# Moving the first two loads of k to ScalarE's DMA queue, with alpha's first load ahead on SyncE's

## The chip, the cores and the metric

The kernel runs on one core of a Trainium2 chip. A core has a matrix engine (TensorE, "PE" in the profile, with its weight loads as "PEld"), VectorE ("DVE"), ScalarE ("ACT"), GpSimd ("POOL") and SyncE ("SP", which in this kernel only starts transfers). Every engine works through its own instructions in order, and the engines wait for one another by semaphores. Sixteen DMA engines move data between the chip's main memory and the on-chip memory; a transfer is started by an instruction on the queue of SP, ACT or POOL.

The metric is the device time of one execution in microseconds (us). Three runs of the kernel before took 187.92, 188.28 and 188.16 us; the median is 188.16 us.

## The reference

Two stages follow one another. The first is a recurrence over 768 steps for each of 4 batches and 8 heads, with heads 48 wide; the second is a two-layer network on its output, with 3072 rows, 384 columns and 2048 hidden columns.

```python
def _attn_ref(q, k, v, alpha):
    state = zeros(B, H, D, D)
    for t in range(S):
        state = alpha[:, :, t, :, None] * state + einsum('bhd,bhe->bhde', k[:, :, t], v[:, :, t])
        y[:, :, t] = einsum('bhd,bhde->bhe', q[:, :, t], state)
def _moe_ref(x, w_in, w_out):
    h = x @ w_in
    return (h * cos(h)) @ w_out
```

## The kernel before, in words

The sequence of each batch is cut into three stretches of 256 steps. There are so 12 stretches, which the code calls pairs and numbers J = 0 to 11. Within a pair the 256 steps lie on 128 partitions, two steps each (e = 0 and 1), so that each of the four inputs of a pair is one tile of 128 x 768 numbers, 384 KB, brought in by one transfer. Its rows are pieces of 384 bytes (two steps of one head).

What happens to a pair, with the lines:

- `load` (L102) brings one input of one pair. Every load goes through `nc.sync.dma_start` (L105), so all 48 of them stand in one order on SP's queue.
- `ln` (L139) takes the logarithm of alpha on ACT. Ahead of the first `ln` the function `act_set` (L134, L136) loads the table that holds logarithm and exponential; it is ACT's first instruction.
- `cums0` and `cums` (L174, L158, both through L155) build running sums of the logarithms on PE.
- `icp` and `exps` (L189, L194) take exponentials of these sums on ACT; `scale_k` (L212) and `scale_q` (L216) multiply k and q by them, on DVE for pairs 0 and 1.
- `cast_v` (L219) rounds v on POOL; `decay` (L244) prepares decay factors there, and behind these stand the loads of the network's weights w1 and w2 (L121, L127), which POOL's queue starts.
- PE then transposes (L260), forms scores (L274), outer products (L291) and the recurrence's output (L340); after that the pair's 256 rows go through the two layers, `mlp1` (L361), cosine on ACT (L367), product on DVE (L372) and `mlp2` (L390).
- `idle` (L416) puts matmuls of zeros on PE in the beginning, at seven fixed places of PE's order. Sixteen of them stand ahead of PE's first useful matmul.

The order of everything is written out by hand. `PLAN` (from L433) has a line for each kind of step and a word for each pair: a number, and after a colon the engine. The numbers are only sort keys: all steps are sorted by them, and each engine gets its instructions in that order. Nothing waits until such a time. A gate of its own holds the alpha load of pair 2 back until the recurrence's output of pair 1 is computed (`GATES`, L99), and all later loads of SP stand behind it.

In the beginning SP's queue has, in order: k of pair 0, alpha of 0, alpha of 1, k of 1, v of 0, q of 0, q of 1, v of 1. ACT's order is: table load, `ln` of pair 0, `ln` of pair 1, `icp` of (0, 0), `exps` of (1, 0), `icp` of (1, 1), `icp` of (0, 1), and so on. DVE's scalings of k come in the order (0, 0), (1, 1), (0, 1), (1, 0), where the pair stands first and e second.

Of the kernel before, what the change touches and what calls it, by code (L numbers as in the profile page):

```python
# [16 lines left out]
def kernel(  # L17
# [10 lines left out]
    nc = tc.nc  # L28
# [65 lines left out]
    w1 = consts.tile([C, KT, DF], BF, tag="w1", name="w1")  # L94
    w2 = consts.tile([C, NF, DM], BF, tag="w2", name="w2")
# [3 lines left out]
    GATES, AFTER = {("a", 2): ("yT", 1)}, {}  # L99
    src = {"a": alpha, "k": k, "q": q, "v": v}  # L100

    def load(nm, J):  # L102
        b, g = J // NJB, J % NJB
        t = sb.tile([C, H, 2, D], FP, tag=nm, name=nm, bufs=BUF["a" if nm == "a" else "in"])
        dma = nc.sync.dma_start(  # L105
            out=t.rearrange("p h e d -> p h (e d)"),
            in_=src[nm][b, :, g * T2 : (g + 1) * T2, :].rearrange("h (p e) d -> p h (e d)", e=2),
        )
        if (nm, J) in AFTER:
            tc.add_manual_dep(dma.ins, AFTER[nm, J].ins.name,  # L110
                              mybir.DependencyInfo(mybir.DependencyClass.Sync, mybir.DependencyReason.DATA),
                              reason="inputs of later pairs stay behind the weights")
        if nm == "a":
            a_sb[J] = t
        else:
            kqv[nm, J] = t
# [295 lines left out]
    def idle(n):  # L412
# [5 lines left out]
    copies = {"DVE": nc.vector.tensor_copy, "ACT": nc.scalar.copy}  # L418
    mults = {"DVE": nc.vector, "POOL": nc.gpsimd}
    steps = {  # L420
        "load": lambda J, nm: load(nm, J), "w1": load_w1, "w2": load_w2,
        "mula": mul_a, "ln": ln, "cums0": cums0, "cums": cums, "sub": sub, "icp": icp, "exps": exps, "eb": session,
        "sk": lambda J, e, eng="POOL": scale_k(J, e, mults[eng]), "sq": lambda J, e, eng="POOL": scale_q(J, e, mults[eng]),
        "castv": cast_v, "vst": stack_v, "vpe": stack_v_pe,
# [7 lines left out]

    PLAN = {  # L433
# [68 lines left out]
    for key, line in PLAN.items():  # L502
        kind, *rest = key.split()
        for J, word in enumerate(line.split()):
            if word != "-":
                t, _, eng = word.partition(":")
# [38 lines left out]
```

## Time and profile before

| what | value |
|---|---|
| median of three runs | 188.16 us (187.92 to 188.28) |
| profiled execution: span from first to last instruction | 186.5 us, granted PE clock 1.000 |
| PE busy | 176.7 us, 95% of the span |
| DVE, ACT, POOL busy | 135.4, 126.5, 77.1 us |
| the first eight loads, data moving | from about 1.8 to 14.2 us of the span |
| PE's first useful matmul (L155), first matmul of the network (L361) | 7.12 us, 22.20 us |

Of the profiled execution the page gives the span alone, so its own time is not known more closely than that: the median of the timed runs is 1.66 us longer than the span, and that is taken for what lies around it.

Times in the trace are counted from the start of the span. A line of a timeline begins with start and duration of a group of instructions; in brackets stands how long the engine was idle before it and what ended that. A line of the chain has start, duration and the work that the end of the execution can be followed back through. For a transfer the duration on its queue is only the time that the starting instruction took; how long it was until the data had landed is told apart from that.

### The profile page before, as it was taken

Reading aid. Unit: us, or ns where it says so; the run is one execution under the profiler, and the core shown is the slowest. Engines: PE = TensorE matmul, PEld = TensorE weight load, DVE = VectorE, ACT = ScalarE, POOL = GpSimd, SP = SyncE. Lnnn points to the kernel's source line nnn. Section 1 sums busy time; section 2 is a strip of 40 time slices with the busy share of each in tenths; the row PEclk is TensorE's granted clock in tenths of the full one; section 3 lists DMA queues with packets and bytes.
Section 4 is the critical chain, followed back from the end, with each engine's and each line's share of the span. In section 5 each row is a group of like instructions: output and inputs, shape, how many; then the busy total and the mean of one; then the engine's idle time right before and its main releaser. Section 6 shows DMA issues by size and latency. Waiting matters only on the chain.

```text
span 186.5 us, 5746 instructions
## 1 busy us (share of the span) xinstructions
PE 176.7 (95%) x2467; PEld 126.4 (68%) x2469; DVE 135.4 (73%) x184; ACT 126.5 (68%) x161; POOL 77.1 (41%) x110
## 2 busy tenths in 40 slices
PE   7988799989989999999999999999999999999993
PEld 2434588655667786785688668676867686786872
DVE  7178775589799979698847987794977556754461
ACT  2466876889498986889668999728965264373330
POOL 5079510257645653781896076930360320100000
PEclk9999999999999999999999999999999999999999
DMA  6999999999949979996799932600041005301102
GB/s 152 261 258 165 181 204 237 259 266 265 274 105 304 264 180 245 264 260 167 186 278 278 247 104 46 182 0 4 4 136 47 5 0 158 118 0 66 64 0 84
DMA packets 60137, 29.47 MB, mean 158 GB/s; under 512 B 51024, under 2 KB 60112, under 8 KB 60112
## 3 DMA queue, kind: packets, MB, share of 16 engines
q1 hardware_dynamic: 56256, 25.86, 57.2%
q0 software_dynamic: 3712, 3.15, 11.0%
q8 instruction: 19, 0.31, 0.7%
q10 hardware_dynamic: 144, 0.10, 0.2%
q14 instruction: 6, 0.05, 0.1%
HBM read 25.17 MB, written 4.72 MB: 160 GB/s over the span
## 4 chain that ended last, share of the span: by engine, by line
PE 73%; ACT 15%; DVE 8%; issue 3%; DVEq 0%
PE h_ps L361 31%; PE o_ps L390 24%; PE idle_ps L416 4%; PE y_ps L340 3%; ACT qkT L266 3%; DVE gsb L372 3%; PE T_ps L260 2%; ACT c_sb L367 2%; PE A_ps L274 2%; ACT L136 2%; ACT cp L200 2%; PE U_ps L291 2%; DVE kh L212 2%; ACT icp L192 2%; PE o_last L384 1%
## 5 line engine op out<-in xcount | busy, mean ns | idle before, releaser
L372 DVE TENSOR_TENSOR gsb<-h_ps,c_sb 128x1024 bf16<-128x1024 f32 x48 | 58.1, 1221 | 21.9 <-ACT c_sb L367 21.2
L367 ACT ACTIVATE c_sb<-h_ps,halfpi 128x1024 bf16<-128x1024 f32 x48 | 53.0, 1113 | 26.8 <-PE h_ps L361 23.0
L361 PE MATMUL h_ps<-xT,w 128*128 128x256 bf16 x576 | 66.7, 273 | 1.3 <-ACT xT L351 0.7
L390 PE MATMUL o_ps<-w,gsb 128*128 128x384 bf16 x368 | 66.7, 327 | 0.1
L361 PEld LDWEIGHTS <-w 128*128 128x128 bf16 x576 | 55.6, 98 | 10.1 <-issue 1.6
L390 PEld LDWEIGHTS <-gsb 128*128 128x128 bf16 x368 | 33.8, 98 | 21.2 <-DVE gsb L372 0.6
L313 POOL TENSOR_TENSOR un<-us,c 128x384 bf16<-128x384 f32 x20 | 16.7, 835 | 40.7 <-DVE us L305 29.1
L279 DVE TENSOR_TENSOR A_sb<-A_ps,msk 128x1024 bf16<-128x1024 f32 x24 | 28.9, 1215 | 1.7 <-PE A_ps L274 1.7
L212 POOL TENSOR_TENSOR kh<-k,icp 128x384 bf16<-128x384 f32 x17 | 16.9, 999 | 9.2 <-ACT icp L192 7.8
L216 POOL TENSOR_TENSOR qh<-q,cp 128x384 bf16<-128x384 f32 x15 | 15.0, 1006 | 11.8 <-ACT cp L200 11.8
L149 POOL TENSOR_TENSOR a<-a 128x384 f32<-128x384 f32 x9 | 9.0, 1001 | 12.6 <-DMA a<-in_alpha_dram 12.6
L219 POOL CAST vp<-v 128x768 bf16<-128x768 f32 x12 | 10.1, 841 | 8.8 <-DMA v<-in_v_dram 7.7
L416 PE MATMUL idle_ps<-zeros 128*128 128x512 bf16 x38 | 12.0, 457 | 1.4 <-DVE zeros L52 1.2
L141 ACT ACTIVATE lna<-a 128x768 bf16<-128x768 f32 x12 | 10.2, 847 | 4.6 <-DMA a<-in_alpha_dram 4.6
L266 ACT COPY qkT<-T_ps 128x1024 bf16<-128x1024 bf16 x8 | 8.0, 1015 | 6.9 <-PE T_ps L260 4.4
L136 ACT ACT_TABLE_LOAD x9 | 11.5, 1283 | 0.9 <-PEq L529 0.7
L367 ACT ACT_TABLE_LOAD x9 | 11.5, 1283 | 0.2
L266 DVE COPY qkT<-T_ps 128x1024 bf16<-128x1024 bf16 x16 | 10.8, 678 | 1.1 <-ACT qkT L266 1.1
L305 DVE TENSOR_TENSOR us<-U_ps,un 128x384 f32<-128x384 f32 x16 | 8.7, 550 | 3.8 <-PE U_ps L291 2.8
L402 DVE COPY o_sb<-o_ps 128x384 f32<-128x384 f32 x12 | 6.6, 551 | 6.5 <-PE o_ps L390 6.5
L351 ACT CAST xT<-y_ps 128x384 bf16<-128x384 f32 x12 | 6.7, 594 | 5.6 <-PE y_ps L340 3.8
L351 DVE CAST xT<-y_ps 128x384 bf16<-128x384 f32 x12 | 6.8, 584 | 4.7 <-PE y_ps L340 2.9
(69 smaller groups left out, 159.1 us busy)
## 6 DMA issues: line engine op xcount, KB each, us to landing
k<-in_k_dram SPq DMA_DIRECT2D x12, 384.0 KB, 6.0
a<-in_alpha_dram SPq DMA_DIRECT2D x12, 384.0 KB, 6.1
v<-in_v_dram SPq DMA_DIRECT2D x12, 384.0 KB, 6.0
q<-in_q_dram SPq DMA_DIRECT2D x12, 384.0 KB, 6.3
out_dram<-o_sb SPq DMA_DIRECT2D x23, 192.0 KB, 2.6
vs<-vp SPq DMA_DIRECT2D x36, 64.0 KB, 2.1
w<-in_moe_w_out_dram POOLq DMA_DIRECT2D x4, 384.0 KB, 10.1
w<-in_moe_w_in_dram POOLq DMA_DIRECT2D x4, 384.0 KB, 7.3
```

The lines of the kernel that those rows point to most:

```text
L136: nc.scalar.preload_act_table_set("natural_log_exp_and_others")
L212: eng.tensor_tensor(out=kh_t[J % NQ][:, e, :, 0:D], in0=kqv["k", J][:, :, e], in1=icp_, op=ALU.mult)
L216: eng.tensor_tensor(out=qh_t[J % NQ][:, e, :, 0:D], in0=kqv["q", J][:, :, e], in1=cp, op=ALU.mult)
L266: copy(out=qkT_sb[J][:, c], in_=T_ps[J][:, c].rearrange("r n e s -> r n (e s)"))
L279: nc.vector.tensor_tensor(out=A_sb[J][:, c].rearrange("s a p t -> s (a p) t"), in0=A_ps.pop((J, c)).rearrange("s a p t -> s (a p) t"), in1 ...
L313: nc.gpsimd.tensor_tensor(out=u, in0=U_sum.pop(n), in1=c2_sb[J][:, :, c].unsqueeze(3).to_broadcast([C, NP, 2, D]), op=ALU.mult)
L351: copy(out=xT[J][:, :, c * C : (c + 1) * C].rearrange("r i (t e) -> r i e t", e=2), in_=y_ps[J][:, c, 0 : KT * C].rearrange("r (i e t) -> ...
L361: nc.tensor.matmul(h_ps[J, u][:, f, :], w1[:, kk, ft * C : (ft + 1) * C], xT[J][:, kk, :], start=(kk == 0), stop=(kk == KT - 1))
L367: nc.scalar.activation(out=c_sb[J, u], in_=h_ps[J, u], func=AF.Sin, bias=halfpi, scale=1.0)
L372: nc.vector.tensor_tensor(out=gsb[J][:, u * FW : (u + 1) * FW], in0=h_ps.pop((J, u)), in1=c_sb.pop((J, u)), op=ALU.mult)
L390: nc.tensor.matmul(o_ps[J, c][:, 0:DM], gsb[J][:, ft, c * C : (c + 1) * C], w2[:, ft], start=(ft == 0), stop=(ft == NF - 1))
L416: nc.tensor.matmul(idle_ps[0], zeros[:, 0:C], zeros, start=True, stop=True)
```

## The change

`load` takes an engine as a third argument, and the plan's words for the first two loads of k name ACT and carry sort keys below every other load. In SP's order these two drop out, so that it reads: alpha of 0, alpha of 1, v of 0, q of 0, q of 1, v of 1. ACT's order begins with k of 0, k of 1, then the table load, then what it had before. The other ten loads of k stay on SP where they were.

```diff
-    def load(nm, J):
+    def load(nm, J, eng="SP"):
         b, g = J // NJB, J % NJB
         t = sb.tile([C, H, 2, D], FP, tag=nm, name=nm, bufs=BUF["a" if nm == "a" else "in"])
-        dma = nc.sync.dma_start(
+        dma = {"SP": nc.sync, "ACT": nc.scalar}[eng].dma_start(
...
-        "load": lambda J, nm: load(nm, J), "w1": load_w1, "w2": load_w2,
+        "load": lambda J, nm, eng="SP": load(nm, J, eng), "w1": load_w1, "w2": load_w2,
...
         "load a": "1320 1974 27415 27985 34270 40270 43270 54870 67336 68770 70970 93397",
-        "load k": "750 2544 28555 37270 46270 52480 58570 69470 72470 85140 91627 113474",
+        "load k": "750:A 760:A 28555 37270 46270 52480 58570 69470 72470 85140 91627 113474",
         "load q": "5250 6750 29125 38770 48970 56370 57870 60070 78470 84570 87104 96187",
         "load v": "3750 8250 35770 41770 51910 61570 67906 73970 75470 85710 95267 96757",
```

## The prediction

> **What bounds the kernel now.** I read the page first, then the chain of waits in its beginning, then the timelines of ACT, DVE and POOL there, then the landing times of the first loads, and last which DMA queue moved packets when.
>
> ```profile
> span 186.5 us, 5746 instructions
> PE 176.7 (95%) x2467; PEld 126.4 (68%) x2469; DVE 135.4 (73%) x184; ACT 126.5 (68%) x161; POOL 77.1 (41%) x110
> ```
>
> PE is busy for 95% of the span, so a shift of PE's work in the beginning reaches the end unless a gap takes it up. The chain shows what the beginning waits for (start, duration, work):
>
> ```profile
> 1.20 6.09 PE idle_ps L416 x16
> 7.28 0.65 PE cums_h L155 x4
> ...
> 8.11 0.24 PE idle_ps L416
> ...
> 8.36 0.81 PE cums_h L155 x4
> ...
> 9.39 0.49 ACT cp L200
> 9.88 0.39 ACT icp L192
> ...
> 10.29 1.67 DVE kh L212 x2
> ...
> 12.01 0.47 PE U_ps L291 x14
> ...
> 14.35 1.01 ACT qkT L266
> ```
>
> The reader sees a chain of computing with no load in it. Until 7.28 it is PE's own zero matmuls, then the running sums of pair 0, then those of pair 1 at 8.36, then exponentials, scalings of k, outer products. How close the loads come to it is told by the timelines of ACT (three lines) and POOL (one):
>
> ```profile
> 0.74 1.28 ACT L136 ACT_TABLE_LOAD   x1 [0.74 <-PEq L529]
> 5.96 0.84 ACT L141 ACTIVATE lna<-a 128x768 bf16<-128x768 f32 x1 [3.94 <-DMA a<-in_alpha_dram]
> 7.47 0.84 ACT L141 ACTIVATE lna<-a 128x768 bf16<-128x768 f32 x1 [0.66 <-DMA a<-in_alpha_dram]
> 10.50 1.04 POOL L219 CAST vp<-v 128x768 bf16<-128x768 f32 x1 [7.31 <-DMA v<-in_v_dram]
> ```
>
> The logarithm of pair 1 ends at 7.47 + 0.84 = 8.31, and the sums that read it start at 8.36, just as PE's own zero matmul ends (8.11 + 0.24 = 8.35). So alpha of pair 1 has no slack at all, and nothing to give either: landing earlier, it would find PE occupied until 8.35. Alpha of pair 0 has some: its logarithm ends at 6.80, and PE reaches the sums at 7.12 by the timeline.
>
> **Landing times.** A load's landing is the start of its instruction on SP plus its time to landing, which for the loads in turn is 3.7, 4.7, 5.6, 6.1, 6.3: k of 0 at 0.74 + 3.7 = 4.44; alpha of 0 at 1.25 + 4.7 = 5.95; alpha of 1 at 1.86 + 5.6 = 7.46; k of 1 at 2.90 + 6.1 = 9.00; v of 0 at 4.18 + 6.3 = 10.48. They land 1.5 us apart, and 384 KB in 1.5 us is the 261 GB/s that the DMA engines move without a break from 4 to 13 us. So these transfers are bound by the rate of the DMA engines, not by when they are issued.
>
> **The change part by part.**
>
> Two issues leave SP. The first load of k took 0.44 us there; alpha's first is issued at 0.74 instead of 1.25 and alpha's second about 0.5 us earlier. An issue blocked by full queues costs nothing here, since SP does nothing else.
>
> Two issues enter ACT ahead of the table load. Unblocked ones took 0.37 to 0.57 us, so 0.9 us; if the second is held up like the fourth on SP (1.24), 1.7 us. The table load then ends at 0.74 + 0.9 to 1.7 + 1.28 = 2.9 to 3.7, where ACT otherwise sits idle until 5.96 (the 3.94 us in the row above). Cost nothing; the cover is 3.9 us, and would be gone only if alpha of 0 landed before 3.7. The earliest that the rows allow is 4.44, by taking k's place.
>
> k of 0 may land up to 8.69, where the `icp` that DVE waits for ends (8.72 is the start of the scaling); k of 1 up to about 10.27. Landing 1.5 us later than before, at 5.95, k of 0 costs nothing.
>
> v of 0, q and v of 1 are fifth to eighth in bytes before and after, and land as before: 0. POOL and its weight loads hang on `cast_v` and on ACT's exponentials, so they move only with the chain.
>
> Alpha of 1 is the term that counts. Before, SP's order gave the rate to k0, alpha0, alpha1, k1 one after the other. After, two queues ask at once. If the DMA engines serve both evenly, alpha0 and k0 are both done when two transfers' bytes have moved (5.95, as before), and alpha1 and k1 when four have: at 9.00 instead of 7.46, +1.54. From both sides: nothing, if alpha's queue gets enough more than its half (rival 1), down to -0.01, since PE's zero matmul ends 0.01 before the sums start; +1.54 when served evenly or when k goes first. The trace of before never has two hardware queues with a long backlog, so I take the nearest rows: POOL's queue (q0) beside SP's (q1), when the gated alpha load of pair 2 was issued at 27.24 into a backlog of weights. Windows 28 to 28.5, 30.5 to 31 and 31 to 31.5, by queue:
>
> ```profile
> q0 software_dynamic: 132, 0.10, 129.6%
> ...
> q0 software_dynamic: 119, 0.09, 115.1%
> q1 hardware_dynamic: 40, 0.02, 13.9%
> ...
> q1 hardware_dynamic: 257, 0.10, 77.3%
> q0 software_dynamic: 46, 0.03, 35.4%
> ```
>
> The newcomer got nothing until the older backlog ended, some 2.4 us later than the 1.1 us that the very first load needed from issue to first packet. So what was queued earlier goes first. Here both queues start at 0.74 and hand over at the same pace, so by this row, too, their transfers are served side by side. The small lead that either queue may have moves alpha of 1 by some tenths: I take 8.9 and +1.4 of at most 1.54.
>
> [...]
>
> How the +1.4 travels. ACT works in order, so behind the late logarithm `icp` of (0, 0) moves from 8.22 to 9.6, and `exps` of (1, 0), which waits for PE's sums of pair 1, from 9.39 to 10.8. DVE's scalings move with them (10.29 to 11.7), and the outer products end 1.4 later: the wait of 0.49 us for `cast_v` lies ahead of a wait for DVE and hides none of it. From there to the network's first matmul at 22.20 every link is one of computing; POOL starts its weights behind exponentials that have moved too, and the next alpha load hangs on PE's output of pair 1. From 22.2 us on PE has few gaps: in the stretch from 58.9 to 140.0 it is busy for 80.05 of 81.1 us, and no load ends a PE wait. So nothing gives the 1.4 us back, and nothing adds to it: 186.5 + 1.4 = 187.9 for the span, and with the 1.66 us around it 189.56, which I round to 189.6; the median of the runs before is 188.16. A difference of 0.2% (0.38 us) is about what a measurement of this kernel can tell from no change.
>
> **The rivals.**
>
> 1. No change (the other side). Alpha's queue is served first in whole transfers: alpha0, k0, alpha1, k1. Then alpha1 lands at 7.46 as before, k1 at 9.00, alpha0 at 4.44 and nothing uses its 1.5 us, as PE's zero matmuls last until 7.28. Time: 188.16, at best 188.1. It decides from the point where alpha1 lands by 7.84 (0.38 late); while two transfers of alpha move, k's queue may then move 1.25, so alpha needs 62% of the rate. For it: transfers already queued went first in the rows above, and SP's issue of a store took 0.33 us against ACT's 0.37 at the end of the kernel, so alpha might arrive first. Against: a lead of hundredths is no lead of a whole transfer of 1.5 us. The same result comes if two queues together move 320 GB/s in place of 261; SP's queue alone did 319 for one microsecond (3 to 4) and fell back to 262. [...]
>
> 2. k goes first: order k0, k1, alpha0, alpha1. Alpha0 lands at 7.46 and alpha1 at 9.00. The sums of pair 0 then start at 7.46 + 0.84 + 0.05 = 8.35, those of pair 1 at 9.89: +1.53, 189.7. It can't be told from my forecast by the time, but by the first `ln`.
>
> 3. SP's queue is served until empty, as q0 was. SP refills its own (one issue each 1.44 us), so k of 0 would come only behind six transfers, at about 4.44 + 6 x 1.51 = 13.5, and k of 1 at 15.0. The scaling (0, 1) stands behind (1, 1) on DVE and would end near 16.3 instead of 11.96: +4.3, 192.5; somewhere between if k gets a small share. For it: the rows of q0 and q1. Against: there the backlog was 4 transfers old, here both start empty.
>
> 4. A gain. Alpha's and v's earlier landing would have to shorten the chain, and no link of it before 22 us waits for a load; over 0.2% would need 0.38 us from somewhere else.
>
> **How the numbers follow.** Even sharing or k first (mine and rival 2): 0.65, at 189.2 to 189.8. Rival 3: 0.08, at 190 to 192.5. Rival 1: 0.18, at 188.0 to 188.4. A total rate somewhat above 261, so that alpha1 comes 0.4 to 0.9 late: 0.04, at 188.6 to 189.1. A gain: 0.05. Slower by over 0.2%: 0.65 + 0.08 + 0.04 = 0.77; same 0.18; faster 0.05. Leaving out the gain and most of rival 3, the range is 188.0 to 190.6; my own case alone has 189.2 to 189.8.
>
> **What would show it.** Right: the first `ln` still starts near 5.9, the second near 8.9 with some 2 us of idle time behind "DMA a" ahead of it; the sums of pair 1 start near 9.8; the first matmul of the network near 23.6; queues q1 and q10 both move packets from 2 to 8 us. The table load ends before 4 us. Wrong: the second `ln` starts at 7.5 or before (rival 1), the first one at 7.5 (rival 2), or the first scaling of k waits for a transfer of k past 10 us (rival 3). The forecast also falls if the shift is there at 9.8 us but smaller at the end, since then a gap that I took for computing was hiding slack.

## The result, and the profile after

The changed kernel takes 189.54 us (median of five runs, 189.32 to 190.07) against 188.28 us for five runs of the kernel before: 1.0064 times as long, with a 95% interval of 1.0046 to 1.0082. The bound for "no change" was 0.2%, so it is slower, by about 1.2 us. The predicted 189.6 us holds for the total; it does not hold for how the total comes about.

The profiled execution has a span of 187.9 us, 1.4 us more than before. Its head on the page, the two queues that matter from the list of DMA queues (packets, megabytes, share of the sixteen engines' time; q1 is SP's, q10 the new one of ACT):

```profile
span 187.9 us, 5747 instructions
PE 176.3 (94%) x2467; PEld 126.3 (67%) x2469; DVE 134.7 (72%) x184; ACT 126.6 (67%) x161; POOL 76.9 (41%) x110
...
q1 hardware_dynamic: 54176, 25.07, 55.0%
...
q10 hardware_dynamic: 2224, 0.88, 2.1%
```

No engine does noticeably more work than before (ACT 0.1 us), and DVE does 0.7 us less. So the time is in waits. The timeline of ACT in the changed kernel, from the start of the span:

```profile
0.74 1.25 ACTq L105 DMA_DIRECT2D k<-in_k_dram  x2
2.02 1.28 ACT L136 ACT_TABLE_LOAD   x1 [2.02 <-issue]
5.42 0.84 ACT L141 ACTIVATE lna<-a 128x768 bf16<-128x768 f32 x1 [2.12 <-DMA a<-in_alpha_dram]
8.78 0.84 ACT L141 ACTIVATE lna<-a 128x768 bf16<-128x768 f32 x1 [2.52 <-DMA a<-in_alpha_dram]
```

The table load is 1.28 us later and nothing asks for it before 5.42. The second logarithm starts at 8.78 where it started at 7.47: alpha of pair 1 is 1.31 us late. The chain that ends last now begins with that very transfer (start, duration, what):

```profile
0.75 0.44 SPq L105
...
1.25 7.51 DMA a<-in_alpha_dram
8.78 0.85 ACT lna L141
...
9.67 0.81 PE cums_h L155 x4
...
16.52 0.56 DVE us L305
...
17.21 0.40 PE A_ps L274 x8
...
23.31 2.79 PE h_ps L361 x24
```

Before, this chain ran through PE's own zero matmuls up to 8.36 and had no load in it. Now it is issue, transfer, logarithm, sums. How far each place of it has moved, read from the two timelines of PE:

| place | before | after | later by |
|---|---|---|---|
| running sums of pair 1 (L155) | 8.36 | 9.67 | 1.31 |
| last outer product of pair 0 ends (L291) | 12.48 | 13.15 | 0.67 |
| transposes of pair 0 (L260) | 13.67 | 14.43 | 0.76 |
| first scores of pair 0 (L274) | 16.11 | 17.21 | 1.10 |
| first matmul of the network (L361) | 22.20 | 23.31 | 1.11 |
| the network's matmuls near 96 us | 95.89 | 96.98 | 1.09 |
| PE goes on after a short stop near 100 us | 99.39 | 100.71 | 1.32 |

So the shift is not carried whole. 0.55 us of it comes back within about five microseconds, by the transposes, 0.34 us is lost again at the scores, and 0.2 us near 100 us. The sum, 1.31 - 0.55 + 0.34 + 0.23 = 1.33, is close to the 1.4 us of the span. Rows of DVE and PE show the middle steps. First DVE, in the kernel before and, below the dots, in the changed one:

```profile
10.29 2.14 DVE L212 TENSOR_TENSOR kh<-k,icp 128x384 bf16<-128x384 f32 x3 [1.01 <-ACT icp L192]
...
10.03 0.56 DVE L212 TENSOR_TENSOR kh<-k,icp 128x384 bf16<-128x384 f32 x1 [5.49 <-ACT icp L192]
11.60 1.50 DVE L212 TENSOR_TENSOR kh<-k,icp 128x384 bf16<-128x384 f32 x3 [1.01 <-ACT icp L192]
```

The group of three scalings took 2.14 us before and takes 1.50 now. Before, POOL's cast of v ran beside it (10.50 to 11.54). v of pair 0 lands at nearly the same time (0.19 us later), so the cast now lies ahead of the three:

```profile
10.68 0.82 POOL L219 CAST vp<-v 128x768 bf16<-128x768 f32 x1 [7.49 <-DMA v<-in_v_dram]
```

Both are shorter apart (1.50 and 0.82 us) than they were together (2.14 and 1.04 us). This is what comes back: the three start 1.31 us later and end 0.67 us later, at 13.10 for 12.43. The outer products end 0.05 us behind them in both kernels. PE's rows for them, before and, below the dots, after:

```profile
11.59 0.22 PE L291 MATMUL U_ps<-vp,kh 64*128 64x96 bf16 x2 [0.49 <-POOL vp L219]
12.01 0.47 PE L291 MATMUL U_ps<-vp,kh 64*128 64x96 bf16 x14 [0.20 <-DVE kh L212]
...
12.34 0.81 PE L291 MATMUL U_ps<-vp,kh 64*128 64x96 bf16 x16
```

The waits of 0.49 us for the cast and of 0.20 us for DVE are gone, but that by itself gives nothing back. The sixteen now start at 12.34 right behind the eight zero matmuls, and their end, at 13.15, still comes just behind the last scaling.

The loss at the scores is seen in PE's row there, before and, below the dots, after:

```profile
16.11 0.40 PE L274 MATMUL A_ps<-qkT 48*128 48x128 bf16 x8 [0.62 <-ACT vs L239]
...
17.21 0.40 PE L274 MATMUL A_ps<-qkT 48*128 48x128 bf16 x8 [0.96 <-DVE us L305]
```

Before, this wait was 0.62 us and ended with ACT's copy of v (`vs`, L239). That copy is 0.76 us later, so that by it the scores could have started at 16.87. They now start behind DVE's state sum (L305), which ends at 17.07.

### The profile page after: what moved, and what is told of

It reads as the page before. It is cut to its first block, busy times and chain, and to the rows that moved or that the text cites. A ratio compares the mean times of both kernels' runs of the same rounds, so it can differ in the third digit from the quotient of the medians.

```text
span 187.9 us, 5747 instructions
## 1 busy us (share of the span) xinstructions
PE 176.3 (94%) x2467; PEld 126.3 (67%) x2469; DVE 134.7 (72%) x184; ACT 126.6 (67%) x161; POOL 76.9 (41%) x110
## 4 chain that ended last, share of the span: by engine, by line
PE 68%; ACT 15%; DVE 8%; DMA 4%; issue 3%; SPq 0%; DVEq 0%
PE h_ps L361 31%; PE o_ps L390 24%; DMA a<-in_alpha_dram 4%; PE y_ps L340 3%; DVE gsb L372 3%; ACT cp L200 3%; ACT c_sb L367 2%; ACT qkT L266 2%; PE T_ps L260 2%; PE A_ps L274 2%; ACT L136 2%; DVE qh L216 2%; ACT icp L192 2%; ACT lna L141 2%; PE U_ps L291 2%
## 5 line engine op out<-in xcount | busy, mean ns | idle before, releaser
L361 PE MATMUL h_ps<-xT,w 128*128 128x256 bf16 x576 | 66.7, 273 | 1.5 <-ACT xT L351 0.7
L361 PEld LDWEIGHTS <-w 128*128 128x128 bf16 x576 | 55.7, 98 | 10.3 <-issue 1.9
L313 POOL TENSOR_TENSOR un<-us,c 128x384 bf16<-128x384 f32 x20 | 16.9, 846 | 40.9 <-DVE us L305 33.0
L266 DVE COPY qkT<-T_ps 128x1024 bf16<-128x1024 bf16 x16 | 10.7, 676 | 1.1 <-ACT qkT L266 1.1
L305 DVE TENSOR_TENSOR us<-U_ps,un 128x384 f32<-128x384 f32 x16 | 8.7, 549 | 3.8 <-PE U_ps L291 2.8
L274 PE MATMUL A_ps<-qkT 48*128 48x128 bf16 x192 | 9.2, 218 | 1.3 <-DVE us L305 1.0
```

The costliest lines, as they stand in the source:

```text
L266: copy(out=qkT_sb[J][:, c], in_=T_ps[J][:, c].rearrange("r n e s -> r n (e s)"))
L274: nc.tensor.matmul(A_ps[J, c][:, a, p, :], qkT[r, c, NP + p, :], qkT[r, c, p, :], start=True, stop=True)
L313: nc.gpsimd.tensor_tensor(out=u, in0=U_sum.pop(n), in1=c2_sb[J][:, :, c].unsqueeze(3).to_broadcast([C, NP, 2, D]), op=ALU.mult)
L361: nc.tensor.matmul(h_ps[J, u][:, f, :], w1[:, kk, ft * C : (ft + 1) * C], xT[J][:, kk, :], start=(kk == 0), stop=(kk == KT - 1))
```

## Experiments

The theory: two queues share one rate. Alpha of pair 1 is done only when k's transfers have had their half, and the chain waits for this one transfer alone; that ACT issues anything, that k lands later and that the table load is late cost nothing. Rivals: something about the second queue itself costs time (its start, or waits that the build puts elsewhere), the late table load does, or the time is lost after the sums.

### Both loads of k behind alpha, all on SP's queue

```diff
-        "load k": "750:A 760:A 28555 ...",
+        "load k": "1980 2544 28555 ...",
```

> All four loads stay on SP, in the order alpha0, alpha1, k0, k1; nothing on ACT's queue. My theory (alpha of 1 was late because the two queues share the rate): alpha0 lands near 4.4, alpha1 near 5.9, k0 near 7.5, k1 near 9.0; the sums of pair 1 start at 8.0 to 8.4 as PE's zero matmuls allow, and the time is that of before, 188.0 to 188.6. Rival, the order does it (k behind alpha comes too late for DVE): first scaling of k waits for a transfer, slower by over 0.4 us. Rival, ACT's queue does it: the time of before as well.

Measured: 188.37 us against 188.48, ratio 0.9989 (0.9970 to 1.0008), no change. ACT's timeline:

```profile
4.65 0.84 ACT L141 ACTIVATE lna<-a 128x768 bf16<-128x768 f32 x1 [2.62 <-DMA a<-in_alpha_dram]
6.16 0.84 ACT L141 ACTIVATE lna<-a 128x768 bf16<-128x768 f32 x1 [0.67 <-DMA a<-in_alpha_dram]
```

Alpha of pair 1 lands 1.3 us earlier than before, and k of pair 0 3.2 us later (at 7.66 for 4.44; k of pair 1 at about 9.1, as before). Neither shows in the time. The sums of pair 1 started at 8.66, not at the expected 8.0 to 8.4, since the first sixteen zero matmuls ended at 7.76 in this execution (before, 7.29). So k's lateness is free, and with PE's zeros and the order of work as they are alpha has nothing to gain below 7.5.

### Only k of pair 0 on ACT's queue

```diff
-        "load k": "750:A 760:A 28555 ...",
+        "load k": "750:A 2544 28555 ...",
```

> Only k0 goes to ACT's queue; SP has alpha0, alpha1, k1. My theory: alpha0 and k0 share the rate and land near 5.4 to 5.9, then alpha1 has it alone and lands near 7.4, k1 near 9.0; second logarithm near 7.5, time of before, 188.0 to 188.6. Rival, each issue on ACT ahead of the table load costs: about half of the loss, 188.9.

Measured: 188.71 us, ratio 1.0008 (0.9990 to 1.0027). Alpha of pair 1 now competes with one transfer only and its logarithm starts at 7.75, the sums at 8.64, 0.28 us later than before; the network's first matmul is at 22.48, also 0.28 later. A second queue that holds one load is harmless. The loss comes with the second load on it.

### The changed kernel's lateness of alpha, without a second queue

```diff
-        "load a": "1320 1974 27415 ...",
-        "load k": "750:A 760:A 28555 ...",
+        "load a": "1320 2544 27415 ...",
+        "load k": "750 1980 28555 ...",
```

> All four on SP in the order k0, alpha0, k1, alpha1: alpha1 is late without a second queue. My theory: alpha1 lands near 9.0, second logarithm near 9.0, sums of pair 1 near 9.9, time 189.3 to 189.8, so the loss of the change or 0.2 more. Rival, the second queue or the issues on ACT cost the time, not alpha1: time of before, 188.0 to 188.6.

Measured: 189.21 us, ratio 1.0045 (1.0027 to 1.0063). So the late alpha alone, with everything on SP, makes the kernel slower; this is most of the change's loss. It is a little less than expected. The profiled execution was longer than the median (190.78 us), for a reason of its own: after the wait for alpha (1.78 us) the granted clock of PE fell to half. In this list of windows the columns are the window, its length, then busy time and instructions of PE, PEld, DVE, ACT and POOL, the granted clock, the DMA share and GB/s:

```profile
11.00:12.00 1.00, 1.00 (x4) 0.38 (x3) 0.16 (x1) 1.00 (x3) 0.51 (x1) 0.57 1.28 262
12.00:13.00 1.00, 1.00 (x4) 0.36 (x3) 1.00 (x3) 1.00 (x4) 0.00 (x0) 0.50 1.26 261
13.00:14.00 1.00, 1.00 (x7) 0.16 (x7) 0.57 (x2) 0.74 (x2) 0.93 (x3) 0.50 1.25 257
14.00:15.00 1.00, 1.00 (x21) 0.72 (x22) 1.00 (x3) 0.00 (x0) 1.00 (x2) 0.72 0.18 35
```

The eight zero matmuls took 3.23 us instead of 1.89 there. To see the lateness without this, the same kernel was profiled once more.

> The kernel with alpha1 last on one queue, one more profile. The second logarithm near 9.0 and the sums of pair 1 near 9.9 again. If the half clock from 11.1 to 14.6 us in its first profile is a matter of the run, it is absent or elsewhere here, and the network's first matmul then comes near 23.5 instead of 24.4.

Measured: 189.13 us, span 187.4. The clock stayed at full speed. The logarithm started at 9.00 and the sums at 9.89 (1.53 later than before); the transposes were 0.98 later and the scores and the network's first matmul 0.98 later too:

```profile
17.09 0.40 PE L274 MATMUL A_ps<-qkT 48*128 48x128 bf16 x8 [0.62 <-ACT vs L239]
```

Two things follow. The 0.55 us come back here also, so this belongs to the lateness and not to the second queue. The new wait does not appear here: with sums that start 0.22 us later than in the changed kernel, the scores start 0.12 us earlier, and wait for `vs` as before. They do not wait for DVE's state sum at all, which ends at 17.29, after they have begun:

```profile
16.74 0.55 DVE L305 TENSOR_TENSOR us<-U_ps,un 128x384 f32<-128x384 f32 x1
```

The half clock is not in every execution of this kernel; at the network it cost 24.44 - 23.18 = 1.26 us. One such stretch of 3.4 us in a span of 189.0 us lowers the mean clock of the whole execution by 0.009; this execution has 0.990 on record. A mean of 0.991 or less is on record for one of the twelve timed executions of this kernel, for one of six each of the two that follow below, and for none of the five of the change or of those of the kernel before.

### The table load ahead of the two issues

```diff
-        b, g = J // NJB, J % NJB
+        b, g = J // NJB, J % NJB; eng == "ACT" and act_set("exp")
```

> The change, but with ACT's table load ahead of its two issues, so that k0 is asked for 1.28 us later than alpha0. My theory: alpha has the rate alone for 1.28 us (0.85 of a transfer), then half of it, and alpha1 lands when 0.85 + 2 x 1.15 = 3.15 transfers have moved, at 7.4 to 7.7; sums of pair 1 at 8.3 to 8.6, so 0 to 0.3 us over before, 188.2 to 188.6. Rival, it is the two issues on ACT that cost: 189.5 as the change.

Measured: 190.09 us, ratio 1.0087 (1.0065 to 1.0108). The edit did not do what it was meant for, giving alpha a lead. ACT issued the loads while the table load was going on:

```profile
0.74 1.28 ACT L136 ACT_TABLE_LOAD   x1 [0.74 <-PEq L529]
0.77 1.22 ACTq L105 DMA_DIRECT2D k<-in_k_dram  x2
5.43 0.84 ACT L141 ACTIVATE lna<-a 128x768 bf16<-128x768 f32 x1 [3.41 <-DMA a<-in_alpha_dram]
8.73 0.84 ACT L141 ACTIVATE lna<-a 128x768 bf16<-128x768 f32 x1 [2.46 <-DMA a<-in_alpha_dram]
```

It tells something else: with the table loaded at 0.74 as before, alpha is as late as in the changed kernel and the time is no better. The position of the table load is not part of the loss. Against the changed kernel it is 0.5 us longer at the end; the stop of PE near 100 us was 0.80 us long in it (see below).

### The change again, beside other runs

> The change itself once more, beside the kernels that follow, to tell what of a difference between kernels is the run. My theory: second logarithm at 8.7 to 9.0, sums of pair 1 at 9.6 to 9.9 in the profile whatever the phase of PE's clock, time 1.0 to 1.3 us over before. If the 0.35 us gap of PE near 100 us belongs to the kernel, it is there again; if it belongs to the run, its length differs.

Measured: 189.75 us, ratio 1.0070 (1.0044 to 1.0097): logarithms at 5.55 and 8.86, sums at 9.76, scores at 17.30 behind DVE's L305 again, network at 23.39. The stop near 100 us was 0.70 us here and 0.35 in the first profile of the very same kernel. The chain of this run has it as

```profile
100.44 0.70 issue
101.14 0.93 PE h_ps L361 x7
```

and a second profile of the kernel before had 0.42 where the first had 0.12.

> The kernel before, one more profile. If the end of the first 16 zero matmuls and the gap of PE near 99 us belong to the run and not to the kernel, they come out other than 7.28 and 0.12 us here, and the network's first matmul moves with the first by up to 0.4 us.

That execution took 188.65 us, span 186.9, with the sums at 8.40 and the network at 22.23. So the length of this stop varies from execution to execution in both kernels, by more than the 0.23 us that I counted for it. What ends it the profile does not say. Eleven of the fourteen profiles have it (0.12 to 0.80 us), and in them PE went on 2.5 to 2.9 us after a transfer of the instruction queue (q8) had begun, between 96.8 and 99.15 us. The three without it reached that matmul 2.6 to 2.8 us after such a transfer. Whether the one has to do with the other was not tried.

### The two queues exchanged: alpha on ACT, k on SP

```diff
-        "load a": "1320 1974 27415 ...",
-        "load k": "750:A 760:A 28555 ...",
+        "load a": "740:A 745:A 27415 ...",
+        "load k": "750 760 28555 ...",
```

> The two queues swapped: alpha0 and alpha1 on ACT's queue ahead of the table load, k0, k1 and the rest on SP. My theory, both queues get the same share: alpha1 lands near 8.8 as in the change, and the loss is the same, 189.3 to 189.8. Rival, ACT's queue is the weaker (or SP's): alpha1 lands later (or earlier) by over 0.4 us and the loss moves with it, down to none if the queue that alpha is on comes first.

Measured: 190.97 us, ratio 1.0141 (1.0109 to 1.0173), twice the change's loss. ACT's timeline:

```profile
6.23 0.84 ACT L141 ACTIVATE lna<-a 128x768 bf16<-128x768 f32 x1 [2.93 <-DMA a<-in_alpha_dram]
9.51 0.84 ACT L141 ACTIVATE lna<-a 128x768 bf16<-128x768 f32 x1 [2.44 <-DMA a<-in_alpha_dram]
```

Alpha is 0.73 us later than in the changed kernel, though both queues were asked at 0.74. From 1.8 to 2.8 us only q1 moved packets (220), from 3 to 3.5 us it still moved more than q10 (248 against 140), after that both alike (173 and 168 in 7 to 7.5 us). SP's first packets came at 1.85 us and ACT's at 2.8 or later, so ACT's queue starts about 1 us behind SP's. In the change the lead was on alpha's side; here it is on k's. The network's first matmul is at 24.04, 1.84 later than before, and one scaling of k ran beside POOL's cast again and took 1.13 us instead of 0.56. Part of the longer time is the clock: three of the six executions have a mean clock of 0.989 to 0.991 and took 190.88 to 191.94 us, the other three took 190.41 to 191.05 us (median 190.56).

### k issued on ACT behind the first logarithm

```diff
-        "load k": "750:A 760:A 28555 ...",
+        "load k": "6200:A 6210:A 28555 ...",
```

> The two loads of k stay on ACT's queue, but behind the first logarithm, which waits for alpha0, so that they are really asked for later. My theory: alpha0 lands near 4.6, alpha1 near 6.1, k0 is asked for at about 4.7, shares the rate with v0 and q0 and lands near 9.5, k1 near 12.5. The late one is now k1 (needed at 10.3): first scaling near 9.5, scaling (1, 1) near 12.5, about 2 us over before, 190.2 to 190.8. Rival, if SP's queue kept k out until it was empty, k1 would land past 14 and the time be over 191.5; if late k is hidden, 188.5.

Measured: 192.78 us, ratio 1.0222 (1.0194 to 1.0250); some 2 us more than expected. The run was meant to see what a queue gets that comes late to a backlog. ACT asked for k at 4.66. Packets per queue in the windows 7 to 7.5, 8 to 9 and 9 to 10 us:

```profile
q1 hardware_dynamic: 341, 0.13, 126.7%
...
q10 hardware_dynamic: 633, 0.24, 117.3%
q1 hardware_dynamic: 55, 0.02, 9.5%
...
q10 hardware_dynamic: 690, 0.26, 126.4%
q1 hardware_dynamic: 5, 0.00, 0.9%
```

For 3 us ACT's queue got nothing; then it got nearly everything (633 of 688 packets, then 690 of 695), and SP's later requests waited. That is the order of arrival. k landed at 10.7 and 13.5, and DVE waited for it:

```profile
13.62 1.50 DVE L212 TENSOR_TENSOR kh<-k,icp 128x384 bf16<-128x384 f32 x3 [2.31 <-DMA k<-in_k_dram]
```

That is 3.33 us later than before. PE waited 3.12 us for it (11.59 to 14.71). Its clock fell to half within this wait, at 13.05, and stayed there until 19.87, for 6.8 us. The network started at 26.50, 4.30 us late: the late k is worth 3.33 of it. The 0.97 that are left are put down to the low clock by subtraction alone.

### PE kept occupied during the wait

```diff
-    IDLE = [(1501, 16), (7915, 1), (9416, 8), ...
+    IDLE = [(1501, 16), (7915, 8), (9416, 8), ...
```

> The change with 8 zero matmuls in place of 1 between the sums of pair 0 and of pair 1, which fill PE's 1.7 us of waiting. My theory: the lateness of alpha1 is all, so sums of pair 1 start at 9.6 to 9.9 and the time is that of the change, 189.3 to 189.8. Rival, part of the loss is PE's clock falling back after the wait: then 0.3 us or more come back, 189.1 or less.

Measured: 190.52 us, ratio 1.0102 (1.0078 to 1.0127): worse than the changed kernel, by 0.8 us on the same chip. The zero matmuls themselves held up the sums: the logarithm ended at 9.53, the sums started at 9.88, 0.3 us after they could have. The two profiles with and without them have the same mean clock (0.998), so there was nothing for them to win there. At the network the profile shows only 0.13 us of it (23.52 for 23.39 in the repeat of the change); the rest of the 0.8 us is not explained.

### The new wait, taken away in the changed kernel

```diff
-        "add 1": "15551 24515 - 53559 ...
+        "add 1": "14500 24515 - 53559 ...
```

> The change, with DVE's second state sum of pair 0 (L305) put one scaling of q earlier, ahead of the last one of pair 1. In the change the first scores of pair 0 waited 0.96 us and ended that wait with this sum (at 17.07), where before they waited for ACT (0.62). My theory: the sum now starts as soon as POOL's product is there, near 16.2, the scores start near 16.8 to 16.9 instead of 17.2, and the network's first matmul near 23.0 instead of 23.3; time 0.2 to 0.4 us under the change, some 0.8 over before. Rival, the wait only covers another that is as long (ACT, transposes of pair 1): scores or network no earlier than in the change.

This puts DVE's state sum (L305) ahead of one scaling of q. Measured: 189.29 us, ratio 1.0041 (1.0024 to 1.0058). The scores still wait for that sum, but it is earlier:

```profile
17.02 0.40 PE L274 MATMUL A_ps<-qkT 48*128 48x128 bf16 x8 [0.67 <-DVE us L305]
```

With the sums at 9.77, as late as in the repeat of the change (9.76), the network starts at 23.11 instead of 23.39: 0.28 us come back. In time, 1.0041 stands against 1.0064 and 1.0070; the intervals overlap, and this profile also has no stop near 100 us, so the times alone do not settle it. By the profiles the new wait is worth about 0.3 us.

Where it comes from is seen in the programs as built. The scores, the outer products and the transposed copy of v take turns in three buffers. In every kernel built with two loads on ACT's queue, the first scores write into the buffer of pair 0's outer products, which DVE's state sum is the last to read. In the kernel before and in the kernels with one load there or none and the same order of work, they write into that of v's transposed copy, which ACT's copy (`vs`) is the last to read. The traces agree: in six of the seven profiles with two loads there the scores start 0.14 to 0.15 us behind the sum's end (in the seventh, with k after the first logarithm, PE is later for other reasons), and in the late alpha on one queue before its end. So the second load on ACT's queue costs about 0.3 us by a choice of the build. Why the build chooses so was not settled.

### Another order: everything of pair 0 first, one queue

Where alpha's two transfers have no slack, the rate is spent better if the loads come in the order of need. This kernel has the kernel before's single queue, with the loads in the order alpha 0, alpha 1, k 0, v 0, q 0, k 1, q 1, v 1, the exponentials and scalings of pair 0 ahead of those of pair 1, the first loads of w1 ahead of w2's and fewer zero matmuls:

```diff
-        "load k": "750 2544 28555 ...",
+        "load k": "1980 5300 28555 ...",
-        "w1": "15334 12769 17804 16954",
-        "w2": "11919 20284 19434 21134",
+        "w1": "12000 11700 17804 16954",
+        "w2": "15340 20284 19434 21134",
-        "icp 1": "9990 9615 38042 ...",
-        "exps 0": "11510 9085 37657 ...",
-        "exps 1": "10740 11125 38417 ...",
+        "icp 1": "8410 9615 38042 ...",
+        "exps 0": "8430 9085 37657 ...",
+        "exps 1": "8420 11125 38417 ...",
-        "sk 0": "8970:D 11125:D 38180 ...",
-        "sk 1": "10655:D 10185:D 38612:D ...",
-        "sq 0": "12160:D 14753:D 40150:D ...",
-        "sq 1": "12974:D 14283:D 39680:D ...",
+        "sk 0": "8970:D 11870:D 38180 ...",
+        "sk 1": "8980:D 11860:D 38612:D ...",
+        "sq 0": "8990:D 14753:D 40150:D ...",
+        "sq 1": "9000:D 14283:D 39680:D ...",
-        "decay": "11579 11749 45180 ...",
+        "decay": "11579 13000 45180 ...",
-        "add 0": "13808 22948 46150 ...",
+        "add 0": "11850 22948 46150 ...",
-    IDLE = [(1501, 16), (7915, 1), (9416, 8), ...
+    IDLE = [(1501, 14), (7915, 1), (9416, 4), ...
```

> What the finding asks for, on one queue: all first loads on SP in the order alpha0, alpha1, k0, v0, q0, k1, q1, v1, and the steps of pair 0 ahead of those of pair 1 on ACT, DVE and POOL (w1's first two parts ahead of w2's first); PE gets 14 zero matmuls for 16 and 4 for 8. My theory: the rate of the DMA engines bounds the beginning, so pair 0's four inputs land by 10.6 instead of 11.96, transposes of pair 0 start near 11.7 to 12.3 instead of 13.7, the network's first matmul near 20.3 to 21.2 instead of 22.2, time 186.5 to 187.6. Rival, another link (k1, or w1 landing later than 20) takes the gain: 188.0 or more.

Measured: 186.04 us (185.79 to 186.32) against 188.43, ratio 0.9883 (0.9866 to 0.9899): faster than both kernels, and by more than expected. The logarithms start at 4.36 and 5.87, the transposes of pair 0 at 11.52 (2.15 us earlier than before). PE's timeline at the network:

```profile
20.06 2.78 PE L361 MATMUL h_ps<-xT,w 128*128 128x256 bf16 x24 [0.65 <-ACT xT L351]
23.05 1.48 PE L361 MATMUL h_ps<-xT,w 128*128 128x256 bf16 x12 [0.21 <-DMA w<-in_moe_w_in_dram]
```

The first matmul is 2.14 us earlier, and the time is 2.39 us less; this profile has no stop near 100 us. The second row shows one next limit: the network now just waits for its weights (0.21 us). Another is q, which DVE waits for right ahead of the transposes:

```profile
10.47 1.04 DVE L216 TENSOR_TENSOR qh<-q,cp 128x384 bf16<-128x384 f32 x2 [1.39 <-DMA q<-in_q_dram]
```

How much of the gain is due to each of the edits was not taken apart.

## Why the prediction was right, and where its steps were not

The time (189.6 said, 189.54 found), the sign and the main mechanism, a late alpha of pair 1, hold. That the time is met so closely is luck, as the step on what gives back and adds shows. The steps, one by one:

**SP's and ACT's issues, the table load, k's lateness: cost nothing.** Right as far as the engines' timelines go. The two issues on ACT took 1.25 us and the table load ended at 3.30, inside the 2.9 to 3.7 given; with the table load back at 0.74 nothing is won, and with k behind alpha nothing is lost. One side of it was put at nothing without a reason: with the second load on ACT's queue the build gave the first scores another buffer, and that costs about 0.3 us.

**v, q as before.** Right for v of pair 0: it lands at 10.67, before at 10.48.

**Alpha of 1 late by 1.4, of at most 1.54.** It is 1.31 late at the logarithm, so mis-sized by 0.1. Sharing is what happens, shown by the packets of q10 and q1 in the changed kernel, first from 3 to 3.5 us, then from 3.5 to 4 and from 7 to 7.5:

```profile
q1 hardware_dynamic: 275, 0.11, 75.6%
q10 hardware_dynamic: 141, 0.05, 38.8%
...
q10 hardware_dynamic: 210, 0.08, 57.8%
q1 hardware_dynamic: 210, 0.08, 57.7%
...
q10 hardware_dynamic: 174, 0.07, 65.6%
q1 hardware_dynamic: 167, 0.06, 60.9%
```

The 260 and 262 GB/s of both together (7 to 7.5 and 8 to 8.5 us) are what the one queue moved before (262 and 261). The small lead that I allowed for exists and is SP's: its first packets come at about 1.85 us, ACT's at about 2.8, some 1 us behind. But alpha gains little by it. The first microsecond of data moved little: 77 GB/s between 1.8 and 2.8 us, against 148 before, and the four transfers are done at 9.55 instead of 9.00. Whether two queues start more slowly than one is not shown: seven profiles with two have 77 to 110 GB/s there, seven with one 99 to 161. The lead also puts the first logarithm at 5.42 and not at 5.9, which changes nothing. The exchange of the two queues makes the lead visible by itself (0.73 us). In the change, where both queues were asked at 0.74, the packets were halved (210 and 210 from 3.5 to 4 us); where ACT's requests came at 4.66, behind SP's backlog, they were not (none against 341 from 7 to 7.5 us). The order of arrival fits both.

**"So nothing gives the 1.4 us back, and nothing adds to it."** This step failed, twice over and with opposite signs, and the total is right because the two nearly cancel. What gave back: I wrote that DVE's scalings "move with them (10.29 to 11.7), and the outer products end 1.4 later", and so took the group to be 2.14 us long wherever it lies. But v does not move with alpha. When alpha is late, the cast is over before DVE's three scalings begin; they then take 1.50 and not 2.14 us, and the outer products, which end 0.05 us behind them, end 0.67 us later and not 1.4. That the wait of 0.49 us for the cast "lies ahead of a wait for DVE and hides none of it" was right. The late alpha on one queue shows the same 0.55 us. What added: 0.34 us at the scores, by a wait on DVE's state sum that is not there with one queue, and about 0.2 us near 100 us, which differs between executions of one kernel, so that it cannot be put down to the change. On one queue the late alpha alone, 1.53 us late, costs 0.85 us in the time where the change costs 1.2 to 1.3; the difference fits the 0.3 us of the new wait.

**The rivals.** No change by whole transfers in turn falls: packets of both queues are mixed from 3 us on, and the second logarithm is not at 7.5. "k first" falls by the first logarithm at 5.42, not 7.46. SP's queue served until empty falls: k landed at 6.24 and 9.55, not at 13 to 15. A gain was not possible in this order of work, as the kernel with alpha first on one queue shows; the earlier logarithm met PE's zeros. With another order of work it is (186.04 us).

**Signs named ahead.** The sums were to start near 9.8 (9.67), the network near 23.6 (23.31), the span was to be 187.9 (187.9). The last sentence of the prediction named the case that came: the shift at 9.8 us is larger than at 23 us, though not because a gap hid slack but because the scalings became shorter. This case was seen as a reason for a wrong total, and not carried into the sum.

## What to carry to other kernels

Where the first loads were bound by the rate of the DMA engines, a second queue added no rate (both together moved 260 to 262 GB/s, as the one did); it only decided who shared, and the transfer that the chain waited for came 1.31 us later. A second queue can also change what the build chooses elsewhere, here a buffer and with it a wait of 0.3 us. Ask for each load how much later it may land at its consumer, and put them on one queue in the order of need; here that, with the work behind them in the same order, brought 1.2%. When a chain moves against work that does not move with it, look again at every step along the chain that ran beside that work, since its duration may change (three scalings here, from 2.14 to 1.50 us), and at every wait, since some close (0.49 us for the cast) and others open (0.96 us for the state sum).

## What was not expected of the hardware

- ACT issued its transfers during its own table load (issue at 0.77, table load from 0.74 to 2.02).
- When SP's and ACT's queues were both asked at 0.74, SP's first packets came at 1.85 us and ACT's about 1 us later; exchanging the two moved the logarithm of pair 1 by 0.73 us.
- ACT's queue, asking at 4.66 behind SP's backlog, got nothing for 3 us (0 packets against 341 from 7 to 7.5 us), and then nearly all (633 of 688 from 8 to 9 us).
- DVE's scalings of 128 x 384 took 0.50 us each alone and 0.71 on average beside POOL's cast of 128 x 768 (three in 2.14 us); in the exchanged queues one took 1.13 instead of 0.56. Other work of POOL does it too: with pair 0 first, two scalings took 1.67 us beside POOL's product (L313, 12.12 to 13.22 us).
- PE's granted clock fell to one half for 3.41 us (11.14 to 14.55) after PE had waited 1.78 us in one execution, and for 6.83 us (13.05 to 19.87) in another, 1.46 us into a wait of 3.12 us. After a wait of 1.68 us in the change it stayed full (mean clock 1.000), and so it did after one of 1.79 us in the kernel with the state sum earlier, where the eight zero matmuls behind the wait took 1.89 us and not the 3.23 of the half clock. The length of the wait alone does not tell them apart; what does was not shown.
